# A fused attention and SwiGLU kernel whose whole instruction order is one list: another list of the same steps

## The chip, the cores and the metric

One core of one Trainium2 chip. The metric is the device time of one execution in microseconds (us). A core has five engines with an instruction stream each: TensorE (PE), VectorE (DVE), ScalarE (ACT), GpSimd (POOL) and SyncE (SP). Each runs its own stream in order and waits on semaphores for what it needs from the others; SP issues transfers, POOL does some elementwise work and issues others.

## The reference

Attention over selected blocks of keys, with a SwiGLU feed-forward network behind it. Batch 4, 8 heads, 768 positions, head size 64; then 3,072 tokens of width 512 and an inner width of 1,536.

```python
k_chunks = k.reshape(B, H, nc, chunk, D)                # chunk = 32, nc = 24
k_min, k_max = np.min(k_chunks, axis=3), np.max(k_chunks, axis=3)
ub = np.sum(np.maximum(q * k_min, q * k_max), axis=-1)  # per query and chunk
ub = np.where(causal, ub, -1000000000.0)
top_chunks = np.argsort(ub, axis=-1)[..., -6:]
scores = scale * np.matmul(q, k.transpose(0, 1, 3, 2))
mask = sel & (pos[:, None] >= pos[None, :])
attn = softmax(np.where(mask, scores, -1000000000.0))
x = np.matmul(attn, v)                                  # to (3072, 512)
xn = x / np.sqrt(np.mean(x * x, axis=-1, keepdims=True) + 1e-06) * rms_g
g = xn @ w_gate
out = (g * (1.0 / (1.0 + np.exp(-g))) * (xn @ w_val)) @ w_out
```

## The kernel before

The unit of the attention part is a pair: two heads of one batch element, 16 pairs in all, four to a batch element. The unit of the feed-forward part is half a batch element, 384 tokens, 8 halves in all. For a pair, k and q are loaded (`kload`, `qload`, L500, issued by SP into one of seven buffers `nat`), transposed on PE (`kT`, `qT`, L520, three tiles a step) and evicted by ACT or DVE (`kE`, `qE`, L290 and L294). DVE takes the minimum and maximum of each chunk of 32 keys (`kmn`, `kmx`, L551 and L549), a small step subtracts them (`dif`, L602), `relu` (L638, or L636 on ACT) makes the positive part of q, and PE forms the bounds (`ub`, L737 for the first six pairs, L795 for two pairs at once afterwards) and transposes them (`up`). DVE adds the causal mask (`ubm`), finds the largest values (`max`, L653) and writes the selection (`sel`, `grd`), which is appended to q as further rows: by a transposition on PE (`selT`, `selC`) for the first three pairs, by transposing DMAs of SP (`qX`, L560) for the others. Casts on POOL or ACT (`kC`, `qC`, `qN`, L294) put k and q in bf16 into one of three buffer sets. Then a pair has twelve score steps (`sc`, L882), an exponential for each on ACT (`exp`, L899), a causal mask on POOL where it is needed (`mask`, L905), the product with v (`av`, L918; v is loaded by POOL, L476) and the division (`xb`, L939).

When the four pairs of a batch element are done, its tokens are normalized (`sq`, `eps`, `root`, `xs`) and transposed: on PE for batch element 0 (`tp`, L1017), by DMAs of SP for the others (`xT`, L1006). Each half then has twelve `gate` steps (L1051) and twelve `val` steps (L1072) of four 128x384 matmuls each, with `tanh` (L1058), `tg` (L1064) and `hh` (L1080) behind them, and nine `po` steps (L1092) of four matmuls of 512 columns, evicted (`poE`) and stored (`out`, L1107). The weights come in six transfers that POOL issues: the first and the second half of the inner width of w_gate (`wg` 76 and 78) and of w_val (`wv` 77 and 79), and w_out (`wo` 80 and 81, L445). Gate and val steps of the first six of the twelve parts read the first half, those of the last six the second. Filler matmuls on zeros (`busy`, L339) may stand anywhere on PE; a list may leave them out.

What sets the order is neither the code's order nor a planner at build time. `add` only records a step, with the engines that it may take, what it depends on and which buffers it opens and uses; its number is the count of the steps recorded before it. Then `Order.run` goes through the string `PROGRAM`, and the steps are emitted as it says. A word is an engine's letter (P, A, D, G for POOL, S for SP), the step's number and, behind a colon, the buffer slots of what it opens: `P347:5,1` is step 347 on PE with PSUM banks 5 and 1. An engine's stream is the words with its letter, in the order of the list. A wait comes of dependencies and of buffers used again, so an instruction that has to wait holds up all that stands behind it on its engine.

Names with the step numbers that are spoken of below: `kload` 559 and 1105, `qload` 227 and 828; `qT` 228 and 230 (pair 2), `ub` 347 and `qX` 356 and 357 (pair 3); `kmn` 410, `kmx` 409, `dif` 411, `kC` 412 (pair 4); `kC` 554 and 555, `dif` 553 (pair 6); `qC` 237 (pair 2), `kC` 343 (pair 3); `gate` 1305 and 1315, `val` 1283, `tp` 1344 (batch element 0); `xT` 1520 (batch element 1); `busy` 28 and 29.

Of the kernel before, what the change touches and what calls it, by code (L numbers as in the profile page):

```python
# [28 lines left out]
    "S83:0 S88:1 S89 S82 D3 G0 D56 D55 D53 D54 D60 G63 A2 G65 P4:0 D59 P5:1 G66 P6:2 D58 P7:3 D57 G67 P8:4 S154:2 "  # L29
    "P9:5 G68 P86:6 S159:3 P10:7 G72 A87:0 P11:0 A69 D97:0 P92:1 D96:0 P12:2 G64 S335:4 G73 P84:3 D93:1 P90:4 A85 "  # L30
    "P13:5 P14:7 A91 P15:6 D95 P16:0 A99:0 P17:2 G101 D94 S222:5 P157:1 P155:5 D98 G62 A158:2 D103:3 P18:3 G61 "
    "P19:7 P20:4 S71 D156 P104:6,0 G102 D1 D52 D165:1 G168:1 P160:2 S330:6 A106:0 P162:3 D164:1 G74 A105 P21:1 "
    "A161:4 P107:7 A163 G167 P336:4 S70 D108:0 P338:5 A171:5 P22:0 G166 D109:2 P23:6 P24:1 A100 D110 S541:0 "
    "P172:2,3 A337:6 D112:0 A339 D111 P225:7 A173:0 D174 P113:0 G346:3 A226:1 S227:1 P175:6 A114 P223:1 D176:1 "
    "P25:4 P26:5 D177:3 P331:2 P333:3 D178 A224 G115:0 S404:2 P119:7 D332:2 A334 P147:6 A179:1 P135:4 D340:4 "
    "A148:0 G170 P128:5 P116:0 A136:1 D180 S399:3 P544:1 A117:2 D341:2 P150:3 P125:2 A545:0 P181:6 P141:4 A151:3 "
    "D232:5 A126:4 P138:0 G342 G236:2 P347:1,3 A120:5 D182 A129:6 G169 P228:2 A139:7 P230:7 S546:5 G183:1 D348:0 "
    "A349 P542:5 D229:5 A231 P350:6 D233:3 A142:8 P190:0 G345:0 P118:1 P121 A239:6 P144:3 P149:2 D351:2 P152 "
    "P184:7 G234 G235 A191:9 D352:6 P240:4,6 D543 A145:2 G238 D353 A185:5 P215:0 P122:5 G251:2 A241:0 D242 P143 "
    "A216:0 P146 P131:3 P243:7 A354 P405:4 A123:3 G237 D244:0 P209:6 P140 P137 A132:8 P218:0 D245:7 P193:7 A210:2 "  # L40
    "G358:3 P407:5 D406:3 A219:7 P203:3 A194:1 D246 P133 P124 P187:6 A408 D248:0 G247 P127 A204:8 P196:0 D153:0 "
    "P402:4 A188:3 P199:7 P217:5 P249:3 D355 A197:4 P130 P212:2 D250 S356:0 P211 A403:4 P195:6 G556:1 P206:0 "
    "A200:0 A213:6 P186 P400:4 G555:1 D134 A207:2 P264:7 P201 S357 P286:3 P214 P277:2 A265:1 G554 D401 P189 "
    "P258:0 P252:1 A278:5 D409:0 G343 P274:7 A259:0 S475:6 P261:4 A253:6 P205 D552:0 P192 G344 P198 P255:2 A275:3 "
    "P271:0 G415:1 D202 A256:8 S470:1 P267:1 P279:7 P220 P208 A287:9 A268:4 P266:2 D551:1 P283:6 A272:5 P288 "
    "P362:3 P257 P276 A262:7 P280:1 S75 D221 P269 P254 P369:0 P260 A281:2 P359:4 G412:2 D410:1 A370:1 P263 P282 "
    "A284:9 P273 P366:5 G76 D270 A363:8 P285 A360:3 P389:1 G77 P371:0 P364:6 P386:3 D329 A367:4 P361 P373:2 "
    "A390:6 G411 D365 G553 P368 P395:4 G78 A387:0 P471:5 D372 P416:7,1 D472:6 A1248:2,0 D1246:1 A1247:2 P379:6 "
    "P478:3 D418:0 A396:7 P547:0 D1249:3 D417 P27:5 A374:2 G1250:4 P397:1 D548:5 P392:4 P476:7 A380:5 P382:5 "
    "P473:2 D1251:0 A383:9 P391 P388 P376:0 A393:1 D1254:1 P375:6 P384 P1252:5 A479:2 P394 D1257:2 P381 A477 "  # L50
    "P1255:4 P419:3 A377:8 D398 G486:0 P1258:7 A1253:0 P378 D1259 P549:0 A1256 D385 P28:1 P29:5 A474 D420:1 "
    "P1260:7 A1336:5,0 D421:7 G413 P1280:1 A1335:1 D480:6 P1268:4 A1337:2 G414:0 D422 A1261:0 P1285:6 D1338:0 "
    "D423 A1281:1 D424 G1339:1 P1270:5 D1262:2 A1286:3 S426 D1282:4 P1275:2 A1271:5 D1346:3 P1263:3 A1276:6 S425 "
    "D1272:7 P1265:7 D1277:0 P1305:1 D1343:0 A1266:1 S559:0 P1288:5 D550 D1264:0 P1344:2 G557:3 P1315:0 D1287:5 "
    "A1345 S564:4 D1267:6 P439:3 A1316:2 P449:6 D1289:1 P445:2 P1300:7 A450:3 D1269:2 P1295:5 G427:0 A440:4 "
    "D481:2 A1301:3 P1283:6 A446:7 D1317:1 G79 A1296:5 P457:4 D1302:6 P560:3 A458:6 P436:2 G482 D1297:2 P1347:0 "
    "G81 A561:1 P562:7 D1348 P565:4 A563 D1284:3 P428:5 P463:3 A437:0 D1340:1 P432:0 G572:0 P487:7,6 A429:2 "
    "D570:3 A464:9 P1273:2 G451 A489:0 D488 A566:4 P1341:5 G485:0 P567:3 A1306:3 D1342 P459:6 A433:1 P490:7 "
    "D1274:4 G430 P1364:4 D569:2 G80 P466:5 P1349:0 A467:5 D491:0 P465 P442:2 D571 D568 P1399:5 A443:8 D1307:5 "
    "P460:7 P452 D575:2 A1400:4 P1278:3 A461:6 D1401:7 P577:2,1 A1350:3 D492:3 A1365:4 D493 G494 P453:7 P1308:5 "  # L60
    "A582:0 D578 A454:9 P1298:1 D1309:5 G455 P583:2 G484:2 D1299:6 P579:7 P462 D1366:5 P456 P1389:5 G434 D581:2 "
    "G483 D580:1 P468 P1392:1 D585 A1390:2 D584 D469:1 G573 P1310:4 D586:4 P1318:7 D592:5 D495 P1402:2 D1351:4 "
    "S496 P1374:6 D1279:7 D1391:3 P438:0 P1354:3 S497 D1393:8 P1303:5 D1403:9 A1355:0 P1367:1 A1375:2 D587 "
    "A1311:3 S700:3 D1319:10 P1290:2 G588 D1356:7 G498:1 P1379:7 D1312:1 A1291:0 P1293:3 D1368:11 A1380:3 G576:2 "
    "D1304:12 P524:4 P1325:1 D1292:5 A525:3 G574:0 D1294:13 P503:5 P444 D1381:6 P510:2 G526 P431 P447 P528:4 D593 "
    "A511:6 P1313:3 D589 A529:9 G594 P435 D1376:0 P703:7 S591 A504:5 P701:2 D1314:14 P1394:4 D595 D702:0 P537:6 "
    "P507:5 S590 P520:3 A538:0 D704 A1395:5 P1326 A521:8 D1396:3 P513:2 G522 S597 P1359:6 A514:2 P539:7 P441 "
    "P499:3 P1327 D448 A500:7 S596 A1360:2 P534:4 G501 P598:2 D1328:0 P1352:0 A535:1 G505 S682:1 A508:0 P516:3 "
    "P523 P506:1 D1353:15 P1384:4 A599:4 D1361:1 A517:8 P530 P536 P531:5 S705:5 D710:7 A1385:5 P512 P509 P665:0 "
    "A532:5 G714:2 P515 P678:2 P527 D1386:4 P672:3 A666:9 P518 P675:6 G558:3 D711:1 S841:2 P533 A673:1 P606:5 "  # L70
    "P502 P669:4 A679:6 P644:0 A676:0 D540 P661:3 G667 P1320:2 A607:2 G713 S823:0 D519 A662:3 P685:6 A670:8 "
    "P674:7 G663 P680 P623:5 D686:5 P657:3 P668 P683:1 G715:1 S687:6 A658:5 A645:7 P671 P1321 D684 A624:1 G646 "
    "D693:2 P648:4 G625 P651:6 S1329 P640:3 A649:6 P654:0 D692:0 P612:1 A641:9 P1322 A613:8 G642 P677 P706:5 "
    "D1323:1 G696:0 A655:0 P650:4 P842:3 S828:4 D707:3 A652:6 P647 P614:1 G712 P609:2 G600 P656 A843:4 P664 "
    "P626:0 P643 A610:7 P653 D681 G694 P633:5 S1324 P708:6 A634:8 P659 P615:3 P601 P826:2 A709 P611 P824:7 S846:3 "
# [1088 lines left out]
```

## Time and profile before

| | us |
|---|---|
| median of 3 runs | 312.94 |
| lowest and highest of them | 311.38, 313.39 |
| the profiled execution: its own time | 312.63 |
| the profiled execution: span from its first to its last instruction | 310.9 |

The granted TensorE clock was 0.999 in the profiled execution. The profile's groups give an instruction's line, engine, operation, what it writes and reads, shapes and count, then busy time and mean duration, then the idle time before it and what ended it. PE's matmuls are pipelined and their ends modelled, so their busy times overlap; the distance from one start to the next says what a step costs.

### The profile page before, as it was taken

Reading aid. Unit: us, or ns where it says so; the run is one execution under the profiler, and the core shown is the slowest. Engines: PE = TensorE matmul, PEld = TensorE weight load, DVE = VectorE, ACT = ScalarE, POOL = GpSimd, SP = SyncE. Lnnn points to the kernel's source line nnn. Section 1 sums busy time; section 2 is a strip of 40 time slices with the busy share of each in tenths; the row PEclk is TensorE's granted clock in tenths of the full one; section 3 lists DMA queues with packets and bytes.
Section 4 is the critical chain, followed back from the end, with each engine's and each line's share of the span. In section 5 each row is a group of like instructions: output and inputs, shape, how many; then the busy total and the mean of one; then the engine's idle time right before and its main releaser. Section 6 shows DMA issues by size and latency. Waiting matters only on the chain.

```text
span 310.9 us, 7415 instructions
## 1 busy us (share of the span) xinstructions
PE 300.8 (97%) x2764; PEld 190.4 (61%) x2782; DVE 232.2 (75%) x651; ACT 182.2 (59%) x405; POOL 119.5 (38%) x176
## 2 busy tenths in 40 slices
PE   7989998999999999999999999999999999999995
PEld 3657875666667764667776456666665455565542
DVE  5888988998977887789987897875743764477621
ACT  5789987672588763866997336667872303433110
POOL 8588856654547840632775104514030110000000
PEclk9999999999999999999999999999999999999999
DMA  9999999999999997996237136533000055200013
GB/s 172 221 170 175 121 209 209 158 168 150 154 176 206 201 163 145 231 163 165 55 26 50 33 74 178 53 74 29 3 0 2 34 86 186 102 2 0 0 70 136
DMA packets 113300, 35.35 MB, mean 114 GB/s; under 512 B 106224, under 2 KB 110064, under 8 KB 113264
## 3 DMA queue, kind: packets, MB, share of 16 engines
q1 hardware_dynamic: 83152, 26.62, 43.0%
q0 software_dynamic: 28512, 7.87, 25.4%
q10 hardware_dynamic: 1600, 0.39, 0.6%
q8 instruction: 22, 0.36, 0.5%
q14 instruction: 14, 0.11, 0.1%
HBM read 28.57 MB, written 6.29 MB: 112 GB/s over the span
## 4 chain that ended last, share of the span: by engine, by line
PE 87%; DMA 8%; POOL 2%; ACT 1%; issue 1%; ACTq 0%; SPq 0%; POOLq 0%
PE vp L1072 20%; PE po L1092 20%; PE gp L1051 19%; PE sc L882 10%; PE av L918 6%; DMA wg<-in_moe_w_gate_dram 5%; PE pq L520 3%; PE pk L520 3%; PE ub L795 2%; DMA knat<-in_k_dram 2%; PE ub L737 1%; DMA qnat<-in_q_dram 1%; POOL ke L294 1%; PE up L817 1%; PE busy L339 1%; POOL rt L638 1%
## 5 line engine op out<-in xcount | busy, mean ns | idle before, releaser
L899 ACT ACTIVATE pt<-sc 128x512 bf16<-128x512 f32 (+1 forms) x192 | 94.0, 556 | 21.2 <-PE sc L882 18.4
L1058 ACT ACTIVATE sg<-gp 128x384 bf16<-128x384 f32 x96 | 45.7, 495 | 72.2 <-PE gp L1051 62.6
L1072 PE MATMUL vp<-xT,wv 128*128 128x384 bf16 x384 | 74.4, 326 | 1.6 <-DMA wv<-in_moe_w_val_dram 1.5
L1051 PE MATMUL gp<-xT,wg 128*128 128x384 bf16 x384 | 74.2, 326 | 0.1
L1092 PE MATMUL po<-wo,hh 128*128 128x512 bf16 x271 | 66.8, 379 | 0.7
L1064 DVE SCALAR_TENSOR_TENSOR tg<-sg,gp 128x384 bf16<-128x384 bf16 x96 | 51.9, 549 | 20.6 <-ACT sg L1058 19.2
L1080 DVE TENSOR_TENSOR hh<-vp,tg 128x384 bf16<-128x384 f32 x96 | 51.5, 552 | 18.5 <-PE vp L1072 17.7
L882 PE MATMUL sc<-qs,ke 128*128 128x128 bf16 (+4 forms) x420 | 59.3, 251 | 0.0
L1072 PEld LDWEIGHTS <-wv 128*128 128x128 bf16 x384 | 35.8, 98 | 26.4 <-DMA wv<-in_moe_w_val_dram 1.8
L1051 PEld LDWEIGHTS <-wg 128*128 128x128 bf16 x384 | 35.7, 98 | 22.5 <-DMA wg<-in_moe_w_gate_dram 0.5
L1092 PEld LDWEIGHTS <-hh 128*128 128x128 bf16 x288 | 27.5, 98 | 27.5
L918 PEld LDWEIGHTS <-pt 128*128 128x128 bf16 x672 | 34.8, 98 | 11.1 <-POOL pt L905 0.3
L918 PE MATMUL av<-vx,pt 128*128 128x65 bf16 x672 | 41.2, 193 | 0.1
L905 POOL TENSOR_SCALAR_AFFINE_SELECT pt<-pt 128x512 bf16<-128x512 bf16 (+1 forms) x48 | 24.5, 522 | 38.5 <-ACT pt L899 38.1
L882 PEld LDWEIGHTS <-ke 89*128 89x128 bf16 (+1 forms) x420 | 31.0, 97 | 10.0 <-issue 1.4
L294 POOL CAST ke<-kt 64x768 bf16<-64x768 f32 x30 | 25.3, 846 | 7.3 <-PE sc L882 2.8
L987 POOL TENSOR_TENSOR ri<-ms,mhalf 128x3 f32<-128x3 f32 x8 | 7.2, 904 | 33.6 <-DVE ms L979 33.5
L995 DVE SCALAR_TENSOR_TENSOR xs<-xb,ri,gains 128x512 bf16<-128x512 bf16 x24 | 17.2, 751 | 3.1 <-POOL ri L987 2.9
L939 DVE TENSOR_TENSOR xb<-av,rden 128x384 bf16<-128x384 f32 (+1 forms) x34 | 18.2, 534 | 1.2
L520 PE MATMUL pk<-ident_f,knat 128*128 128x128 f32 x96 | 16.0, 282 | 1.7 <-DMA knat<-in_k_dram 1.7
L476 POOL DMA_DIRECT2D vx<-in_v_dram x16 | 17.3, 1079 | 0.1
L653 DVE MAX8 m<-ubm 128x8 f32<-128x8 f32 (+4 forms) x192 | 16.8, 160 | 0.2
(91 smaller groups left out, 300.6 us busy)
## 6 DMA issues: line engine op xcount, KB each, us to landing
out_dram<-osb SPq DMA_DIRECT2D x24, 256.0 KB, 2.3
knat<-in_k_dram SPq DMA_DIRECT2D x30, 192.0 KB, 4.4
qnat<-in_q_dram SPq DMA_DIRECT2D x30, 192.0 KB, 5.1
vx<-in_v_dram POOLq DMA_DIRECT2D x16, 192.0 KB, 5.9
wg<-in_moe_w_gate_dram POOLq DMA_DIRECT2D x2, 768.0 KB, 11.7
wv<-in_moe_w_val_dram POOLq DMA_DIRECT2D x2, 768.0 KB, 10.6
wo<-in_moe_w_out_dram POOLq DMA_DIRECT2D x2, 768.0 KB, 11.8
qs<-qn SPq DMA_TRANSPOSE x26, 2.8
```

What stands on the lines that cost most here:

```text
L294: engine[e].tensor_copy(out_, in_)
L520: nc.tensor.transpose(t[:, j * P:(j + 1) * P], nat[w].tile[:, j0 + j].rearrange("p h d -> p (h d)"), ident_f[:])
L882: nc.tensor.matmul(t[:, x:x + m, :].rearrange("p a b -> p (a b)"), ke[kk, kb * P:(kb + 1) * P], qs[kk, q0 * P:(q0 + m) * P], start=not tri ...
L899: nc.scalar.activation(out=t[:, 0:nn, :], in_=sc.tile[:, 0:nn, :], func=ACT.Exp, scale=SCALE)
L905: nc.gpsimd.affine_select(out=pt.tile[:, 0:nd, :], in_=pt.tile[:, 0:nd, :], compare_op=ALU.is_ge, fill=0.0, base=0, pattern=[[0, nd], [1, ...
L918: nc.tensor.matmul(av.tile[:, qi - i0, :], pt.tile[:, x, :], VX[c.v.slot][:, hl * NT + kb, :], start=(begin and m == 0), stop=(left[0] == ...
L1051: nc.tensor.matmul(t[:], wg[:, g, hs], XT[b].tile[:, g, cols], start=(g == 0), stop=(g == NP - 1))
L1058: nc.scalar.activation(out=t[:], in_=gp.tile[:], func=ACT.Tanh, scale=0.5)
L1064: nc.vector.scalar_tensor_tensor(out=t[:], in0=sg.tile[:], scalar=1.0, in1=gp.tile[:], op0=ALU.add, op1=ALU.mult)
L1072: nc.tensor.matmul(t[:], wv[:, g, hs], XT[b].tile[:, g, cols], start=(g == 0), stop=(g == NP - 1))
L1080: nc.vector.tensor_tensor(out=t[:], in0=vp.tile[:], in1=tg.tile[:], op=ALU.mult)
L1092: nc.tensor.matmul(po.tile[:], hhs[ht].tile[:, th * P:(th + 1) * P], wo[:, ht, :], start=(ht == 0), stop=(ht == NHT - 1))
```

## The change

`PROGRAM` is replaced by another list over the same recorded steps; nothing else in the file differs. The new list has 1,876 words, the old one 1,878: `busy` 28 and 29 are not in the new one, which leaves 24 fillers of 26. All other steps are in both. Steps that two engines may take are shared out anew in part: of the evictions `kE` ACT has 16 of 32 (was 19) and `qE` 21 (was 20), of `poE` 9 of 24 (was 12), of `ubE` 17 of 22 (was 12), of `sq` 18 of 24 (was 17), of `relu` 7 (was 6), and `grd` has 6 on ACT, 2 on DVE and 8 on POOL (was 3, 4 and 9). The slots of buffers differ throughout, and almost every line of the list does. Some lines of the two lists:

```diff
 PROGRAM = (
-    "S83:0 S88:1 S89 S82 D3 G0 D56 D55 D53 D54 D60 G63 A2 G65 P4:0 D59 P5:1 G66 P6:2 D58 P7:3 D57 G67 P8:4 S154:2 "
...
-    "D232:5 A126:4 P138:0 G342 G236:2 P347:1,3 A120:5 D182 A129:6 G169 P228:2 A139:7 P230:7 S546:5 G183:1 D348:0 "
...
-    "P402:4 A188:3 P199:7 P217:5 P249:3 D355 A197:4 P130 P212:2 D250 S356:0 P211 A403:4 P195:6 G556:1 P206:0 "
-    "A200:0 A213:6 P186 P400:4 G555:1 D134 A207:2 P264:7 P201 S357 P286:3 P214 P277:2 A265:1 G554 D401 P189 "
-    "P258:0 P252:1 A278:5 D409:0 G343 P274:7 A259:0 S475:6 P261:4 A253:6 P205 D552:0 P192 G344 P198 P255:2 A275:3 "
...
-    "P362:3 P257 P276 A262:7 P280:1 S75 D221 P269 P254 P369:0 P260 A281:2 P359:4 G412:2 D410:1 A370:1 P263 P282 "
-    "A284:9 P273 P366:5 G76 D270 A363:8 P285 A360:3 P389:1 G77 P371:0 P364:6 P386:3 D329 A367:4 P361 P373:2 "
-    "A390:6 G411 D365 G553 P368 P395:4 G78 A387:0 P471:5 D372 P416:7,1 D472:6 A1248:2,0 D1246:1 A1247:2 P379:6 "
...
-    "D1272:7 P1265:7 D1277:0 P1305:1 D1343:0 A1266:1 S559:0 P1288:5 D550 D1264:0 P1344:2 G557:3 P1315:0 D1287:5 "
...
-    "D481:2 A1301:3 P1283:6 A446:7 D1317:1 G79 A1296:5 P457:4 D1302:6 P560:3 A458:6 P436:2 G482 D1297:2 P1347:0 "
...
-    "D1431:3 P1372:5 D1398:21 P1409:7 S1432 D1388:22 D1373:23 P1419:6 D726 S1105:0 D733:5 P1414:1 D734 D725 P1420 "
...
-    "D1109:4 A1451:1 D1437:2 A754:6 P1416 S1520 A744:9 P755:2 P1106:5 G745 D1417:2 P816:3 G741 P746 S1128:0 "
...
+    "S83:0 S82 S89:1 S88 G0 D3 D55 D53 P4:0 D56 D60 P5:1 A2 G65 P6:2 D59 G64 P7:3 G61 G66 P8:4 S154:2 D52 D54 D57 "
...
+    "P181:1 A120:5 D341:2 P135:4 G169 P116:3 A136:6 D182 G342 P230:6 A123:7 G167 P228:4 S399:4 A231:5 D233:3 "
+    "P347:5,1 G236 A545:4 A229 D543 P184:6 G238 D239:3 A349:0 P138:0 A348 P209:4 G234 A185:8 P350:7 A210:9 P124:1 "
...
+    "P407:5 G354 P152 P215:0 D248:0 A213:4 P199:6 P137 G247 P400:4 A204:3 D408 P402:2 A401:6 D355 G555:0 P214:3 "
...
+    "A188:1 D153:0 P264:4 A207:9 G343:1 S357 S356 P217 P220 P261:0 D134 P267:5 P201:2 A265:2 P258:7 P252:6 G344 "
+    "A268:6 S475:5 D410:0 A259:7 P198 P286:4 P192 P208 P274:1 A253:4 P255:5 D409:0 A287:3 P277:7 A262:0 P260:6 "
+    "S470:6 P186 P266 A256:9 P189 D221 P280:4 G411 G415:0 A278:7 P362:0 P195 P257 P263 A275:8 P269 P366:5 D202 "
+    "S75 P547:3 A363:2 P369:7 A367:1 D551:1 P359:1 A370:5 P283:2 P368:0 G76 A360:9 D548:3 P371 P271:5 A284:0 "
+    "P279:7 G77 P288 P254 P364:1 A281:6 P361 P386:3 D365 A272:1 P382:2 G78 P282 P276 D270 P389:4 A387:5 P376:1 "
+    "P395:5 G412:2 A383:7 P285 D372 P273 P379:3 P392:6 D329 G554 P473:2 A380:3 P471:0 P416:3,7 A1248:2,0 D1247:1 "
...
+    "A1286:3 D1338:0 P1263:0 D1267:4 S426 G1339:2 A1261:5 D1287:6 P1283:3 D1262:7 P1270:6 S425 D1343:3 P1275:4 "
+    "D1346:0 A1271:0 P1344:5 D550 P1315:1 S559:0 A1345 D1284:0 G557:0 P1300:2 A1276:2 D1264:1 A1316:3 P1288:5 "
+    "D1277:5 S564:1 A1301:1 D1317:7 P445:3 P439:0 P1295:4 D1269:2 A440:0 G427:0 D1302:2 P1347:1 A446:1 P1305:7 "
...
+    "S1520 D1442:7 P785:2 D1462:1 P795:1 P792:3 P1415 D1412:0 A796:4 S1105:0 A786:6 D1422:1 P781:0 A793:2 P789:6 "
```

On POOL, the words ahead of the second transfer of gate weights (`G78`) are, from the cast of pair 6 on: before `G555 G554 G343 G344 G415 G412 G76 G77 G411 G553 G78`, after `G555 G237 G343 G344 G411 G415 G76 G77 G78`, with `G412` and `G554` behind. On PE, the steps from the first gate on are, before: gate 1260, 1280, val 1268, gate 1285, 1270, 1275, val 1263, gate 1265, 1305; after: gate 1280, 1260, 1265, 1285, val 1268, 1263, 1283, gate 1270, 1275, tp 1344, gate 1315. On DVE, between the selection of pair 3 and `kmx` 409, before: `selC` 250, `xb` 134, `kE` 401; after: `kE` 403, `selC` 250, `xb` 153 and 134, `kmn` 410. On SP, the k load 1105 stood directly behind the transposes of batch element 1's first half, and now stands behind `xT` 1520 of its second half and four `qX`.

222 rows, old and new, of the table PROGRAM are left out of this document.

## Prediction

> **What bounds the kernel now.** I read the page first, then TensorE's (PE's) waits, the windows (start and end, length, PE's busy time first), the chain of waits back from the end, and GpSimd's (POOL's) timeline at the place to which the chain leads.
>
> ```profile
> span 310.9 us, 7415 instructions
> ```
> ```profile
> PE pk L520 <- DMA knat<-in_k_dram: 1.7, 2, 1.3
> PE vp L1072 <- DMA wv<-in_moe_w_val_dram: 1.5, 1, 1.5
> PE busy L339 <- DVE zeros L334: 1.2, 1, 1.2
> PE pq L520 <- DMA qnat<-in_q_dram: 0.5, 1, 0.5
> PE pq L520 <- ACT pt L899: 0.2, 1, 0.2
> ```
> ```profile
> 0.00:57.00 57.00, 51.65 (x609) 35.46 (x611) 47.24 (x154) 45.57 (x101) 38.98 (x59) 1.00 1.22 179
> 57.00:307.00 250.00, 249.10 (x2157) 154.91 (x2171) 184.94 (x498) 136.08 (x303) 80.53 (x117) 1.00 0.58 97
> ```
>
> The two windows say where PE's time is lost: 249.1 of the 250 us from 57 to 307 are busy, against 51.65 of the first 57. All its waits together are 5.1 us, and the rows below put the wait for wv at 51.90, inside the first 57 us; the others there are for k and q as they come in. So there are two stages: a start that waits for transfers, and 250 us in which PE runs without a pause. In the second stage no order of the same work can gain anything; it can only add waits. What an order can gain is work that PE does before the second stage begins. The chain shows what starts that stage:
>
> ```profile
> 41.31 14.69 DMA wg<-in_moe_w_gate_dram
> 56.04 0.82 PE gp L1051 x4
> ```
> ```profile
> 57.52 0.22 PE tp L1017 x4
> 57.74 0.65 PE gp L1051 x4
> ```
> ```profile
> 33.05 3.35 POOL L294 CAST ke<-kt 64x768 bf16<-64x768 f32 x4 [1.06 <-PE sc L888]
> 36.49 2.14 POOL L638 TENSOR_SCALAR rt<-qt 128x768 f32<-128x768 f32 x1
> 38.57 0.82 POOL L294 CAST ke<-kt 64x768 bf16<-64x768 f32 x1
> 39.34 0.82 POOL L440 DMA_DIRECT2D wg<-in_moe_w_gate_dram  x1
> 40.17 0.75 POOL L440 DMA_DIRECT2D wv<-in_moe_w_val_dram  x1
> 40.92 0.45 POOL L602 TENSOR_TENSOR ku<-kmx,ku 128x24 f32<-128x24 f32 x2
> 41.31 0.79 POOL L440 DMA_DIRECT2D wg<-in_moe_w_gate_dram  x1
> ```
>
> The first two fences are the chain (start, length, what), the third is POOL. POOL is released by a score at 33.05, does four casts of k (0.84 us each), a ReLU and another cast, and only then issues the gate weights, the value weights and the second half of the gate weights. That third transfer takes 14.69 us and lands at 56.0; the first gate step that reads it starts at 56.04, and from there the chain stays on PE. PE meets the weights like this:
>
> ```profile
> 48.51 0.59 PE L339 MATMUL busy<-zeros 128*128 128x512 bf16 x2
> 48.99 1.46 PE L1051 MATMUL gp<-xT,wg 128*128 128x384 bf16 x8
> 51.90 0.82 PE L1072 MATMUL vp<-xT,wv 128*128 128x384 bf16 x4 [1.45 <-DMA wv<-in_moe_w_val_dram]
> 52.56 2.11 PE L1051 MATMUL gp<-xT,wg 128*128 128x384 bf16 x12
> ```
>
> Two filler matmuls, two gate steps of four matmuls, a wait of 1.45 us for wv, then a value step, three gate steps and two more steps up to the one on the late half of wg.
>
> **The change, part by part.** No instruction of the computation goes or comes. The program has 1,876 words instead of 1,878: fillers 28 and 29 are gone. Some eviction-like steps change between ScalarE (ACT) and VectorE (DVE); as PE had no wait for either after 57 us, I cost that at nothing there, the cover being the distance in PE's order between an exponential and its product, which is as short in both programs (the two at their shortest, by PE's own work, stand directly behind one another in both). If that cover fails it costs about one exponential each time, 556 ns:
>
> ```profile
> L899 ACT ACTIVATE pt<-sc 128x512 bf16<-128x512 f32 (+1 forms) x192 | 94.0, 556 | 21.2 <-PE sc L882 18.4
> ```
>
> *Work ahead of the late half of wg.* I compared the lists of PE's steps ahead of the first gate step on that half (step 1305 before, 1315 after). They are the same 172 steps, except that the two fillers are only in the old list, and that the new one has val 1283 and the transposition tp 1344 besides. A step of four 128x384 matmuls takes 0.65 us and a transposition of four 0.22 us (the chain's rows at 57.74 and 57.52). So if that gate step starts at the same 56.04, PE has 0.65 + 0.22 = 0.87 us less left to do. The two fillers are worth 48.99 - 48.51 = 0.48 us, but ahead of a wait: they bring PE to the weights earlier, not to the end.
>
> *Does PE get there in time?* In the new order four gates come first, then three vals, two gates and the tp: 9 x 0.65 + 0.22 = 6.07 us from the first gate to step 1315. With the first gate at 48.99 as before and no wait, 1315 would be reached at 55.06, 0.98 us ahead of the weights. The first value step now stands four steps behind the first gate, not two, which takes 2 x 0.65 = 1.30 of the 1.45 us of wv's wait. So the first gate may slip by 0.98 us before PE, not the weights, sets the end. Two edits can make it slip:
>
> ```profile
> 22.35 0.65 PE L737 MATMUL ub<-qt,ku 64*32 64x256 f32 x12
> 22.81 0.63 PE L737 MATMUL ub<-rt,ku 64*32 64x256 f32 x12
> 23.61 0.85 PE L520 MATMUL pq<-ident_f,qnat 128*128 128x128 f32 x6 [0.18 <-ACT pt L899]
> ```
>
> The bound of pair 3 (ub 347, at 22.35) used to run while PE waited for pair 2's q; now both transpositions of that q (qT 230, 228) stand ahead of it. What is behind on PE is everything, and the selection of pair 3 and its two transposing loads qX 357 and 356 hang on it. The ub rows last 1.0 us together from the first start to 23.4, so at that point PE falls back by up to 1.0 us; at the low end nothing, if q lands sooner. Two fillers fewer give 0.48 us back. I take a slip of 0.5 us, inside the cover of 0.98.
>
> *When do the weights leave?* On POOL, ahead of the weights, the chain's casts kC 554 and kC 412 (0.8 us each by their rows) are put behind the third transfer, as is dif 553; qC 237, another cast of the same size, and dif 411 come in ahead. kC 555 goes to another set of buffers, freed earlier, and the wait for a score is now at kC 343. From 33.05, POOL alone would have two casts, the ReLU and two issues, 1.7 + 2.1 + 1.6 = 5.4 us, and issue the third transfer at 38.5, against 41.31. But dif 411 waits for the maximum kmx 409 on DVE, and DVE does there:
>
> ```profile
> 31.70 0.61 DVE L668 SCALAR_TENSOR_TENSOR qn<-m,ubm 128x288 bf16<-128x288 f32 x1
> 32.34 1.14 DVE L294 COPY qs<-st 64x768 bf16<-64x768 bf16 x2
> 33.40 0.18 DVE L938 RECIPROCAL rden<-av 128x6 f32<-128x6 f32 x1
> 33.61 0.56 DVE L939 TENSOR_TENSOR xb<-av,rden 128x384 bf16<-128x384 f32 x1
> 34.09 0.55 DVE L294 COPY kt<-pk 128x384 f32<-128x384 f32 x1
> 34.74 0.95 DVE L549 TENSOR_REDUCE kmx<-kt 128x24 f32<-128x768 f32 x1
> 35.61 0.94 DVE L551 TENSOR_REDUCE ku<-kt 128x24 f32<-128x768 f32 x1
> ```
>
> After the selection (end 32.31) the new order has a copy kE (0.55), the copies selC (1.1), two norms xb (33.40 to 34.09, 0.69 each), kmn 410 and kmx 409 (0.9 each): 32.31 + 0.55 + 1.1 + 1.4 + 1.8 = 37.1. Then dif 411 (half of 0.45, 0.2), the ReLU (2.1) and the first issue at 39.4, against 39.34; the third, without the two difs between, at 41.0, against 41.31. So the casts taken away are replaced by a wait on DVE. For the landing I take 56.0 again: the bounds are 0.3 us earlier by the issue of the third and 1.0 us later if DVE is as late as PE can make it (below).
>
> ```profile
> DMA packets 4240, 3.28 MB, mean 193 GB/s; under 512 B 2574, under 2 KB 4110, under 8 KB 4238
> ...
> q0 software_dynamic: 1584, 2.36, 79.7%
> ```
>
> These two rows (transfers from 39 to 56 us) say why an earlier issue need not be an earlier landing: the three transfers, 2.36 MB, share 193 GB/s with the last k load, the gains and pair 4's transposes, and 2.36 MB at that rate are 12.2 us. The Trainium skill, DMA: Bandwidth & Descriptors, section Anatomy of one DMA, gives about 2.0 us plus the bytes over 436 GB/s for a transfer issued by GpSimd; as an estimate by that page three transfers of 768 KB would need 2.0 + 5.4 = 7.4 us, no weight would hold PE up, and the sum would be that of the faster rival below. The trace does not agree: 14.69 us.
>
> *Sum.* Start of the late gate step unchanged at 56.0: 0. Work left behind it: -0.87. One new wait of small size in the 250 us: +0.3 (bounds 0 and 3, below). The end is built alike: the last PE step is the last third of an output tile, evicted on ACT and stored. That gives -0.6 on the profiled execution's 312.63 us (span 310.9 and 1.7 around it), 312.0. The runs of before have a median of 312.94, 0.3 above the profiled one; I stay with 312.0.
>
> **Rivals.** *Faster: DVE is done in time and the transfers keep up.* Then the third transfer leaves up to 2.8 us earlier and PE itself is the limit, at 55.06 less the fillers' 0.48, 54.6: 1.46 + 0.87 = 2.3 us, 310.3. For it: the casts are really gone from the chain. Against: DVE's sum above, and the 193 GB/s.
>
> *Slower: the weights leave later because dif 411 holds them.* POOL is in order, and behind dif 411 stand the ReLU and all three transfers. Every microsecond that kmx 409 is later than 37.1 is one at the end, since nothing in the 250 us can take it back; it decides the sign from 37.1 + 0.87 = 38.0 on. A slip of pair 3's chain through PE by the 1.0 us above and again as much on DVE gives 2.0: 312.63 - 0.87 + 2.0 = 313.8.
>
> *Slower: short leads in the 250 us.*
>
> ```profile
> knat<-in_k_dram SPq DMA_DIRECT2D x30, 192.0 KB, 4.4
> ...
> xT<-xs SPq DMA_TRANSPOSE x18, 2.5
> ```
>
> Counting PE's work between a load's place and its first reader, k load 559 has 3.1 us, 1.1 less than before, k load 1105 has 3.9 (was 12.7, and now stands on SP's queue behind xT 1520, which waits for DVE), and the last xT of two halves 2.6. Against 4.4 and 2.5 us to landing these are waits of up to 1.3, 0.5 and twice 0.1, and as much again for what SP holds up behind them: about 3, so 315. Against it: other loads got longer leads (q load 828 11.7 us, was 7.2).
>
> *Nothing: the late gate step comes 0.87 us later for one of these reasons, and all is as it was,* 312.6.
>
> **How the numbers follow.** Forecast 0.45; faster rival 0.15; weights later 0.17; short leads 0.13; nothing 0.10. The range 310.4 to 314.6 leaves out about half of the short leads, the edge of the faster rival, and the tails of the rest, some 2 in 10. A measurement of this kernel can tell about 1% from no change: 309.8 to 316.1. Faster than that needs more than the whole start can give: 0.05. Slower needs short leads with more than three microseconds or two cases together: 0.09. Within: 0.86.
>
> **What would show it.** Right: PE's waits for wv nearly gone, the third weights transfer issued near 41 and landing near 56, no PE wait after it, and the PE window from 57 to the end as full as before. The faster rival shows as an issue near 38 and a gate on the late half before 55.5; the slower one as POOL idle ahead of ku L602 with a releaser on DVE, and an issue after 42. Short leads show as PE waits for knat or xT after 57. The prediction is wrong if PE has waits of over 2 us in all after 57, or if the late gate step starts 2 us from 56.

## The result and the profile after

| | before | after |
|---|---|---|
| median of 22 runs each, us | 312.35 | 313.94 |
| lowest and highest, us | 311.37, 313.91 | 312.61, 319.36 |
| profiled execution: its own time, span, us | 312.63, 310.9 | 313.27, 311.6 |

The ratio of after to before is 1.0051, 95% interval 1.003 to 1.0071: about half a per cent slower, and not the 0.2% faster that was forecast. Ratios here and below leave out runs more than 1.5% above the fastest of the same list (3 of the 22 after), medians and ranges do not; as such long runs come only with the short leads described below, the ratios of those lists understate their loss.

The two windows that carried the prediction, in the profile of after (start and end, length, then PE's busy time first):

```profile
span 311.6 us, 7411 instructions
```
```profile
0.00:57.00 57.00, 50.48 (x603) 35.31 (x606) 46.55 (x150) 43.82 (x98) 40.52 (x63) 1.00 1.10 176
57.00:307.00 250.00, 249.10 (x2160) 155.17 (x2174) 186.07 (x499) 139.26 (x311) 78.36 (x112) 1.00 0.57 99
```

The long stage is as full as before to the second decimal; in the profiled execution PE has no wait in it. The first 57 us have 1.17 us less work in them. PE's waits (us in total, times, longest), of which none lies behind 57:

```profile
PE pk L520 <- DMA knat<-in_k_dram: 3.8, 3, 2.7
PE busy L339 <- DVE zeros L334: 1.2, 1, 1.2
PE sc L882 <- DMA qs<-qn: 1.1, 1, 1.1
PE pq L520 <- DMA qnat<-in_q_dram: 0.2, 1, 0.2
```

The wait for wv is gone, as forecast. In its place stands a wait of 2.7 us for k. The sum of all waits is 6.3 us against 5.1; that is 1.2 us more, and with 0.48 us less of fillers the span should be 0.7 us longer, which it is. PE's timeline shows where:

```profile
45.46 0.85 PE L520 MATMUL pk<-ident_f,knat 128*128 128x128 f32 x6 [2.66 <-DMA knat<-in_k_dram]
...
51.36 2.76 PE L1051 MATMUL gp<-xT,wg 128*128 128x384 bf16 x16
53.95 2.11 PE L1072 MATMUL vp<-xT,wv 128*128 128x384 bf16 x12
55.90 1.46 PE L1051 MATMUL gp<-xT,wg 128*128 128x384 bf16 x8
57.20 0.39 PE L1017 MATMUL tp<-ident_b,xs 128*128 128x128 bf16 x4
57.43 1.46 PE L1051 MATMUL gp<-xT,wg 128*128 128x384 bf16 x8
```

The first row is `kT` 473 of pair 5, which reads `kload` 470. From there PE runs through: first gate at 51.36 (48.99 before), gate 1315 on the late weights at 57.43 (step 1305 at 56.04 before). The weights no longer set that step:

```profile
36.02 0.24 POOL L602 TENSOR_TENSOR ku<-kmx,ku 128x24 f32<-128x24 f32 x1 [2.17 <-DVE rden L938]
36.23 2.13 POOL L638 TENSOR_SCALAR rt<-qt 128x768 f32<-128x768 f32 x1
38.32 0.85 POOL L440 DMA_DIRECT2D wg<-in_moe_w_gate_dram  x1
39.16 0.76 POOL L440 DMA_DIRECT2D wv<-in_moe_w_val_dram  x1
39.89 0.77 POOL L440 DMA_DIRECT2D wg<-in_moe_w_gate_dram  x1
```

They leave at 38.32, 39.16 and 39.89, each 1.0 to 1.4 us earlier than before, and by the trace land at 47.77, 51.64 and 55.37, the last 2.06 us before it is read. The chain of waits (start, length, what) shows what sets the end instead:

```profile
32.79 0.23 PE sc L882 x2
33.02 0.83 POOL ke L294
33.86 0.22 SPq L560
...
34.12 1.66 SPq L560
...
37.04 0.54 SPq L500
...
37.63 7.70 DMA knat<-in_k_dram
45.33 0.14 issue
45.46 0.85 PE pk L520 x6
```

It is read upwards: PE waits for k load 470; its second DMA took 7.70 us; it left at 37.63 because the q load 475 and the transposes `qX` stand ahead of it on SP; and those waited for a cast on POOL and a score on PE. SP's own waits between 25 and 40 us name both:

```profile
SPq L560 <- DVE qn L668: 6.2, 1, 6.2
SPq L560 <- PE sc L882: 1.5, 1, 1.5
SPq L560 <- POOL ke L294: 1.1, 1, 1.1
```

In the profile of before the same stretch has a row for DVE alone (6.9 us). So two things are new: SP waits for a score and for a cast with the loads queued behind, and a load that takes 8.3 us from its first DMA's issue to its landing, where the same load, issued at the same 37.04, took 4.91 before. As the load itself leaves no later than before, what has changed for it is that the weights now follow 1.02 us sooner.

### The profile page after: what moved, and what is told of

It reads as the page before. It is cut to its first block, busy times and chain, and to the rows that moved or that the text cites. A ratio compares the mean times of both kernels' runs of the same rounds, so it can differ in the third digit from the quotient of the medians.

```text
span 311.6 us, 7411 instructions
## 1 busy us (share of the span) xinstructions
PE 299.8 (96%) x2761; PEld 190.5 (61%) x2780; DVE 232.8 (75%) x648; ACT 183.7 (59%) x409; POOL 118.9 (38%) x175
## 3 DMA queue, kind: packets, MB, share of 16 engines
HBM read 28.57 MB, written 6.29 MB: 112 GB/s over the span
## 4 chain that ended last, share of the span: by engine, by line
PE 88%; DMA 6%; SPq 4%; issue 1%; POOL 0%; DVE 0%; ACT 0%; ACTq 0%; DVEq 0%
PE vp L1072 20%; PE gp L1051 20%; PE po L1092 19%; PE sc L882 10%; PE av L918 6%; DMA knat<-in_k_dram 5%; PE pk L520 3%; PE pq L520 3%; SPq L500 2%; PE ub L795 2%; PE ub L737 1%; PE up L817 1%; SPq L560 1%; DMA out_dram<-osb 1%; PE tp L1017 0%
## 5 line engine op out<-in xcount | busy, mean ns | idle before, releaser
L1058 ACT ACTIVATE sg<-gp 128x384 bf16<-128x384 f32 x96 | 45.5, 492 | 61.7 <-PE gp L1051 52.7
L882 PE MATMUL sc<-qs,ke 128*128 128x128 bf16 (+5 forms) x420 | 57.8, 251 | 1.3 <-DMA qs<-qn 1.1
L1092 PEld LDWEIGHTS <-hh 128*128 128x128 bf16 x288 | 27.7, 98 | 28.1
L918 PEld LDWEIGHTS <-pt 128*128 128x128 bf16 x672 | 32.1, 98 | 9.2 <-ACT pt L899 0.4
L882 PEld LDWEIGHTS <-ke 128*128 128x128 bf16 (+1 forms) x420 | 30.9, 97 | 10.5 <-issue 1.8
L918 PE MATMUL av<-vx,pt 128*128 128x65 bf16 x672 | 37.2, 193 | 0.0
L296 DVE TENSOR_SCALAR osb<-po 128x512 f32<-128x512 f32 x15 | 10.2, 688 | 15.7 <-PE po L1092 12.1
```

The source lines that it names most:

```text
L882: nc.tensor.matmul(t[:, x:x + m, :].rearrange("p a b -> p (a b)"), ke[kk, kb * P:(kb + 1) * P], qs[kk, q0 * P:(q0 + m) * P], start=not tri ...
L918: nc.tensor.matmul(av.tile[:, qi - i0, :], pt.tile[:, x, :], VX[c.v.slot][:, hl * NT + kb, :], start=(begin and m == 0), stop=(left[0] == ...
L1058: nc.scalar.activation(out=t[:], in_=gp.tile[:], func=ACT.Tanh, scale=0.5)
L1092: nc.tensor.matmul(po.tile[:], hhs[ht].tile[:, th * P:(th + 1) * P], wo[:, ht, :], start=(ht == 0), stop=(ht == NHT - 1))
```

## The experiments

All ratios are to the kernel before, run beside the list on the same chip; the runs are from four chips, so two edits are compared through their ratios. There are 12 runs of each list unless another number is given. "Lead" is the time from the first DMA of k load 470 to the first weights transfer. Diffs show the words of one engine's stream around the edit. The first run is the changed list once more.

> The changed list as it is, beside the kernel before on the same chip. Expected by every theory: ratio 1.003 to 1.007, PE's wait at the transposition kT 473 (reads k load 470) 2 to 3 us, first gate step near 51.4, late gate step 1315 near 57.4.

Ratio 1.005 (1.0011 to 1.009); median 318.28, from 313.27 to 321.76. By the medians the loss is 1.6%. The wait is there, but in the profiled execution, which is the longest of the 12, it is 7.5 us and not 2 to 3, and the first gate comes later than expected. The wide range is taken up again at the end.

**470 far ahead of the weights.**

```diff
-S399:4 S357 S356 S475:5 S470:6 S75
+S399:4 S475:5 S470:6 S357 S356 S75
```

> The changed list with the q load 475 and the k load 470 put ahead of the transposes qX 357 and 356 on SP, where SP idles from 25 to 32.7 us. Nothing else moves. Theory A (the loss is PE's wait for k load 470, which lands only at 45.3): the load lands before 32, the wait of 2.7 us at kT 473 goes, the first gate step comes near 48.7 and the late gate step 1315 near 55.4, where the third weights transfer becomes the limit; 2.0 us below the changed list, ratio to the kernel before 0.993 to 0.999. Rival B (470's wait only covers other late inputs, so that PE is held up elsewhere in the first 57 us by as much): first gate step within 0.5 us of 51.4, ratio near 1.005. Rival C (the earlier loads take bandwidth from the v loads and qX): new waits of 1 us and more ahead of 38 us, and less than half of the 2.0 us gained.

Ratio 1.0017 (0.9991 to 1.0043). The wait at 473 is gone, but the first gate comes at 51.40, where rival B puts it, and the late one at 57.47. PE's waits name rival C as the reason: `av L918 <- DMA vx` 0.9 us and `sc L882 <- DMA qs` 1.9 us. The loads left at 25.1 to 27.7, among the three v loads of POOL (25.5 to 27.6). v load 183 landed 1.4 us later, PE stood still for it, the scores that `qX` waits for came later, `qX` left at 34.12, and 473 was reached only at 44.63. An idle stretch of a queue is not an idle stretch of what it feeds.

**The weights 0.9 us later.**

```diff
-G411 G415:0 G76 G77 G78 G412:2 G554
+G411 G415:0 G554 G76 G77 G78 G412:2
```

> The changed list with the cast kC 554 put back ahead of the first weights transfer on POOL, as in the list before: the three weights transfers leave about 0.85 us later (39.2, 40.0, 40.7). Theory A1 (k load 470 is late because the weights' transfers now start 1 us earlier, within half a microsecond of its second DMA, and their traffic is served ahead of or beside it): 470 lands near 42.5 instead of 45.3, PE's wait at kT 473 shrinks from 2.7 to below 0.6 us, the late weights land near 56.2 and set the late gate step; 1.2 us below the changed list, ratio 0.998 to 1.002. Rival A2 (470 is late for another reason, such as its buffer, its place on SP's queue or qX beside it): it lands again at 45 to 45.5, and the time is that of the changed list, ratio 1.003 to 1.007.

Ratio 1.0022 (1.0 to 1.0045). A1's mechanism holds: with a lead of 1.72 instead of 1.28 us, 470 lands 4.92 us after its issue, and the first gate comes at 49.87. The size does not: the third weights transfer lands at 57.38 and not at 56.2, and now holds PE:

```profile
49.87 2.76 PE L1051 MATMUL gp<-xT,wg 128*128 128x384 bf16 x16
...
57.43 1.47 PE L1051 MATMUL gp<-xT,wg 128*128 128x384 bf16 x8 [1.30 <-DMA wg<-in_moe_w_gate_dram]
```

**470 ahead of 475, the gains out of the way, and both.**

```diff
-S399:4 S357 S356 S475:5 S470:6 S75
+S399:4 S357 S356 S470:6 S475:5 S75
```

> The changed list with the k load 470 put directly ahead of the q load 475 on SP (both still behind the transposes qX 357 and 356), so that its two DMAs leave at 35.8 and 36.5, more than 1.5 us ahead of the weights. Theory Z (from 39 to 56 us the DMA engines are full at about 210 GB/s, so that what k and q get the weights lose): PE's wait of 2.7 us for knat at kT 473 goes, the first gate step comes at 48.8 to 49.9, but the third weights transfer lands at 56.5 to 57.4 instead of 55.4 and sets the late gate step there; 0 to 0.9 us below the changed list, ratio 1.001 to 1.004. Rival P (the order of the loads alone matters, the weights keep their landing of 55.4): late gate step 55.4, ratio 0.997 to 1.000. Rival Q (the q load 475 takes 470's place as the late one): a wait of 0.5 us or more at its transposes.

```diff
-S399:4 S357 S356 S475:5 S470:6 S75
+S399:4 S75 S357 S356 S475:5 S470:6
```

> The changed list with the load of the gains (256 KB, step 75) put ahead of the transposes qX 357 and 356 on SP, where SP idles from 25 to 32.7 us; it leaves the stretch in which weights and k load 470 move. Theory Z: 256 KB are 1.2 us at 210 GB/s; 470 and the weights land 0.5 to 1.2 us earlier together, the first gate step comes near 50.4, the late gate step near 56.4; 1.0 us below the changed list, ratio 1.000 to 1.003. Rival R (470 is late by its place behind the weights' packets, not by the sum of the bytes): it lands at 45.0 to 45.6 again, and the time is that of the changed list, 1.004 to 1.006.

```diff
-S399:4 S357 S356 S475:5 S470:6 S75
+S399:4 S75 S357 S356 S470:6 S475:5
```

> Both of the two other edits: gains ahead of the transposes, k load 470 directly ahead of q load 475. Theory Z: the wait at kT 473 goes and 256 KB less are moved with the weights; first gate step near 48.8, late gate step near 55.4, so that the work of 0.87 us done ahead of it comes out as a gain: ratio 0.995 to 0.999, about 2 us below the changed list. Rival (sum not limited by DMA but by PE's slip ahead of 38 us, the wait of 1.1 us for qs at sc 362): late gate step at 56.4 or later, ratio 1.001 or more.

Ratios 1.0037 (1.0009 to 1.0065), 1.0035 (1.0006 to 1.0065) and 1.0018 (0.9991 to 1.0045). The first went as theory Z says, with the weights even later than its 56.5 to 57.4: 470 on time, first gate at 49.59, weights at 57.73. In the second 470 landed at 45.68, as rival R says, though the gains were no longer beside it, and PE stood 1.5 us at 473 until then; with the gains in the stretch of the v loads PE also waited for vx (0.6) and `qX` left at 34.14. In the third 475 took 470's place (8.14 us to landing with a lead of 0.63), and PE, not the weights, was late: 1.7 us for qs, 0.9 for vx, late gate 57.02. So in all five of these edits the late gate stayed between 57.0 and 57.8; behind each wait taken away stood another. (One of the 12 runs of the second took 633 us; nothing here explains it.)

**The order of the feed-forward steps alone, in the list before.**

```diff
-P1260:7 P1280:1 P1268:4 P1285:6 P1270:5 P1275:2 P1263:3 P1265:7 P1305:1 P1288:5 P1344:2 P1315:0
+P1260:7 P1280:1 P1285:6 P1270:5 P1268:4 P1275:2 P1263:3 P1265:7 P1288:5 P1344:2 P1305:1 P1315:0
```

> The list before with one part of the change alone, the order of PE's feed-forward steps: the value step 1268 is put behind the gate step 1270, so that four gates stand ahead of it, and the gate step 1305 on the late weights behind val 1288 and the transposition tp 1344. Theory (the step of the prediction: work of 0.87 us is done ahead of the late weights, in the time of wv's wait): wv's wait falls from 1.45 to some 0.3 us, 1305 starts near 56.0 with 0.87 us less left, ratio 0.996 to 0.999. Rival (PE was the limit there, and the moved work only delays 1305): 1305 near 56.8, ratio 0.999 to 1.002.

Ratio 0.9984 (0.9964 to 1.0005), median 0.83 us lower: consistent with a gain of 0.87 us, without excluding none. The trace shows the step: no wait for wv is left, and 1305 starts at 55.23, 0.14 us behind the landing of its weights, and not near 56.0 as expected. It also shows a part handed back, 1.9 us of waits behind 57 in an execution that was the slowest of its 12:

```profile
PE sc L882 <- ACT pt L899: 0.7, 1, 0.7
PE av L918 <- DMA vx<-in_v_dram: 0.5, 1, 0.5
PE pq L520 <- DMA qnat<-in_q_dram: 0.5, 1, 0.5
PE sc L882 <- DMA qs<-qn: 0.2, 1, 0.2
```

**The same order with the gains moved, and the gains alone, in the list before.** The first has the edit above besides this one:

```diff
-S356:0 S357 S475:6 S470:1 S75
+S75 S356:0 S357 S475:6 S470:1
```

> The list before with the order of PE's feed-forward steps changed as in the run of that part alone, and the load of the gains put ahead of the transposes qX 356 and 357. Theory Z: weights land 1 us earlier, no wait for wv or wg is left, PE sets the late gate step at 54.5 to 55.0; ratio 0.994 to 0.998. Rival G (what PE gains at the start is handed back to loads of 57 to 150 us whose landing does not move with it): waits of 1 us and more after 57, ratio 0.998 to 1.000 like the run without the gains moved.

> The list before with one edit: the load of the gains (256 KB) put ahead of the transposes qX 356 and 357 on SP. It separates the two parts of the run in which this edit and the order of the feed-forward steps stood together (0.9952). Theory Z (bytes that leave the stretch from 39 to 56 us bring the weights in earlier): wv's wait falls from 1.45 us to about 0.3 and the late weights land near 54.8; 0.6 to 1.2 us gained, ratio 0.996 to 0.998. Rival (the gains are no part of the weights' 14 us): no change, 0.999 to 1.001, weights at 55.5 to 56.5.

Ratios 0.9952 (0.9927 to 0.9977) and 0.9935 (0.9907 to 0.9964): both faster than the list before. In this list v load 183 leaves at 22.5, well ahead of the gains, so that nothing is held up. wv's wait is 0.2 us in the run of the gains alone, with the late weights at 55.50 rather than the 54.8 expected. The gain of the gains alone (9 runs) is larger than the 0.2 to 0.4% expected; its profiled span, 310.6 us against 310.9 before, shows only a part of it, so where the rest comes from stays open. That run against the one with both edits cannot be told apart by these intervals.

**The order undone, in the changed list.**

```diff
-P1263:0 P1283:3 P1270:6 P1275:4 P1344:5 P1315:1
+P1263:0 P1270:6 P1275:4 P1315:1 P1344:5 P1283:3
```

> The changed list with val 1283 and tp 1344 put behind the gate step 1315, that is without the work of 0.87 us that the prediction counted as a gain. Theory I (in the changed list PE, not the third weights transfer, sets the late step: no wait of PE stands behind kT 473 at 45.5, so the order of its steps behind that is worth nothing): 1315 starts 0.87 us earlier, near 56.6, with 0.87 us more left, ratio as the changed list's, 1.003 to 1.007. Rival (the step still gains its 0.87 us in the changed list): 0.9 us slower than the changed list, ratio 1.006 to 1.010.

Ratio 1.0076 (1.0035 to 1.0117), which doesn't tell the two apart. The trace agrees with theory I: from the first gate at 51.84 PE runs without a wait to 1315 at 57.03 (expected near 56.6), 5.19 us instead of 6.07, with 0.87 us more left behind it. The first gate was 0.5 us later than the changed list's for other reasons (waits for vx and q).

**The wait on SP: which buffer set pair 3 has.** Pair 3's `qX` writes into a set that its cast `kC` 343 or `qX` itself opens: set 0 in the list before, whose last readers are the scores of pair 0, and set 1 in the changed one, read by the scores of pair 1.

With the sets, the casts 343 and 555 trade places on POOL, and later openings of the two sets are exchanged too.

```diff
-G555:0 G237 G343:1 G344
+G343:0 G237 G555:1 G344
...
-G573:1
+G573:0
...
```

> The changed list with two buffer sets exchanged: pair 3 takes set 0 (last read by the scores of pair 0) and pair 6 set 1, instead of 1 and 0, with the casts kC 343 and kC 555 in each other's place on POOL; later openings of the two sets are exchanged too. In the changed list the transposes qX 357 and 356 have their input at 31.1 but wait 1.5 us more for the scores of pair 1 that read set 1, and hold SP's queue with k load 470 in it. Theory S (that wait is the root: SP is late by it, and 470 so runs into the weights): qX leaves near 31.3, the wait of 1.1 us for qs at sc 362 goes, k load 470 leaves near 35.6 and lands by 41, PE's wait at kT 473 goes or is below 0.5 us; first gate step 48.5 to 49.5, late gate step 55.4 to 56.4; ratio 0.996 to 1.001, 1 to 2 us below the changed list. Rival (the loads and the weights still share the DMA engines, and the weights then land late): 470 on time, but the third weights transfer lands at 57 or later, ratio 1.002 or more.

Ratio 0.9933 (0.9905 to 0.996); median 311.43, and 1.2% below the changed list by the two ratios. SP's queue and PE in its profile:

```profile
31.70 2.64 SPq L560 DMA_TRANSPOSE qs<-qn  x2
34.38 2.00 SPq L500 DMA_DIRECT2D qnat<-in_q_dram  x2
36.43 1.22 SPq L500 DMA_DIRECT2D knat<-in_k_dram  x2
```
```profile
42.33 0.82 PE L520 MATMUL pk<-ident_f,knat 128*128 128x128 f32 x6
...
49.09 2.76 PE L1051 MATMUL gp<-xT,wg 128*128 128x384 bf16 x16
51.69 2.11 PE L1072 MATMUL vp<-xT,wv 128*128 128x384 bf16 x12
53.64 1.46 PE L1051 MATMUL gp<-xT,wg 128*128 128x384 bf16 x8
55.33 1.48 PE L1051 MATMUL gp<-xT,wg 128*128 128x384 bf16 x8
```

`qX` leaves 1.05 us earlier (not the 1.4 expected), 470 with a lead of 2.30 us, and it lands in 4.54 us. Of the 1.02 us by which this lead is longer than the changed list's, 0.61 come from 470 (36.43 instead of 37.04) and 0.41 from the weights, which leave later (38.73 instead of 38.32). SP's waits between 25 and 40 us still name a score and a cast, for less time:

```profile
SPq L560 <- PE sc L882: 1.2, 1, 1.2
SPq L560 <- POOL qs L294: 0.6, 1, 0.6
```

So the run shows what a longer lead is worth; it does not tell the set from the place of the two casts. There is no wait at 473, the first gate is at 49.09, and the late one starts with the landing of its weights at 55.33, with the 0.87 us done ahead of it. That is the forecast's mechanism: 0.87 us less left, and the late gate, which the forecast left where it was, 0.7 us earlier than the 56.04 before, 1.6 us together; its profiled span is 1.3 us shorter, 309.6 against 310.9.

**All of it together.** The run before, with `S75` ahead of `S357`, `S470` ahead of `S475`, and on POOL:

```diff
-G167 G236 G238 G234 G183:1
+G167 G183:1 G236 G238 G234
```

> The run with the two sets exchanged, and three edits more: gains ahead of the transposes, k load 470 ahead of q load 475, and the v load 183 two casts earlier on POOL (near 22.7 instead of 25.1), so that the gains don't hold it up. Theory S with Z: no wait over 0.5 us for qs, vx, knat or weights from 22 us on, first gate step 48 to 48.8, late gate step 54.0 to 55.0; ratio 0.990 to 0.996. Rival (the next limit is close behind, PE's and DVE's chain to the first gate): late gate step 55.4 or later, ratio 0.997 or more.

Ratio 0.9945 (0.9921 to 0.997): no better than the exchange of sets alone. The ratio lies in the theory's range, but the late gate is where the rival puts it: the weights land at 54.81, and PE reaches it only at 55.62.

**The lead alone, in the list before.** The two lists differ almost everywhere, so one edit shortens the lead alone, by putting two casts behind the weights:

```diff
-G555:1 G554 G343 G344 G415:1 G412:2 G76 G77 G411 G553 G78
+G555:1 G343 G344 G415:1 G76 G77 G411 G553 G78 G412:2 G554
```

> The list before, with the casts kC 412 and kC 554 put behind the third weights transfer on POOL as in the changed list, and nothing else: the first weights transfer leaves near 37.7 instead of 39.3, 0.7 us behind the first DMA of k load 470 (2.3 us in the list before). Theory C (a k or q load that leaves less than about 1.3 us ahead of the weights lands 7 us and more after its issue instead of 4 to 5): 470 lands at 44 to 46, PE's wait at kT 471 grows from 0.4 us to 2 to 4 us, the first gate step comes near 51 and the late gate step at 56 to 57 although the weights left earlier; ratio 1.000 to 1.006, slower runs among them. Rival D (it is the changed list's other order on SP and PE that makes 470 late): 470 lands near 42, the weights land 1.5 us earlier, wv's wait of 1.45 us goes; ratio 0.994 to 0.997.

Ratio 1.0217 (1.0167 to 1.0268; 6 runs, 11 of the list before): theory C, and far above its size. No wait of PE names the two casts. The weights left at 36.69, a lead of 0.29 us, and 470 landed 12.85 us after its issue:

```profile
49.38 0.87 PE L520 MATMUL pk<-ident_f,knat 128*128 128x128 f32 x3 [8.66 <-DMA knat<-in_k_dram]
```

So letting the weights go 2.65 us earlier cost the list before 2.2%. The leads and landings in these traces, in us:

| run | lead of 470 | 470, issue to landing | third weights transfer, issue to landing |
|---|---|---|---|
| lead shortened in the list before | 0.29 | 12.85 | 15.89 |
| order undone | 0.76 | 7.77 | 15.87 |
| changed list again | 0.85 | 13.11 | 16.31 |
| gains moved in the changed list | 0.97 | 7.07 | 16.16 |
| changed list | 1.28 | 8.29 | 15.47 |
| weights later | 1.72 | 4.92 | 16.54 |
| gains alone, list before | 1.77 | 4.89 | 14.55 |
| both edits, list before | 2.00 | 4.76 | 13.69 |
| 470 ahead of 475 | 2.28 | 4.01 | 17.84 |
| list before | 2.30 | 4.91 | 14.69 |
| sets exchanged | 2.30 | 4.54 | 14.97 |

With a lead of up to 1.28 us the load takes 7 to 13 us, from 1.72 us on 4 to 5; no run lies between. It is the second of the load's two DMAs that is late: in the changed list the first took 4.1 us and the second 7.7. Not in the table are three runs with leads of 1.85, 2.45 and 4.35 us (3.98, 4.97 and 5.07 us to landing) and the first edit, where 470 took 10.99 us among the v loads, far from the weights.

## Why the prediction was wrong

In the prediction's sum, the term "start of the late gate step unchanged" stood at 0 and came to +1.39 (57.43 against 56.04); the 0.87 us came as counted; the new wait in the 250 us, put at +0.3, came to 0. That makes +0.5, and the two profiled executions are 0.64 us apart. Of the signs that the prediction named for being right, four came: wv's wait gone, a landing near 56, no PE wait after 57, a window as full as before. None of the four is on PE's way to the first gate, and there it failed.

**The bound: right.** 249.1 of 250 us are busy after 57 in both lists, with no wait in the profiled execution of after. The short leads in that stage, the slower rival at 315, did not show there.

**The work ahead of the late gate: right as work, not a gain by itself.** The 0.87 us are real where the weights set the late step (sets exchanged: 55.33 with the weights' landing). In the changed list PE sets it, 2.06 us behind the weights, and then the order of PE's steps from 45.5 on is worth nothing. The prediction stated that condition and believed it met.

**"The first gate may slip by 0.98 us ... I take a slip of 0.5 us, inside the cover": this is the step that failed.** The slip was 51.36 - 48.99 = 2.37 us. It did not come from the two edits that the prediction named (the bound behind two transpositions, two fillers): with the wait for 470 gone the first gate came at 49.09, 49.55, 49.59 and 49.87 in four runs, slips of 0.1 to 0.9, within the cover (in two others, the first edit and the one with both moves on SP, waits for v and `qX` took its place). It came from k load 470, which the prediction did not cost at all. Its row of 193 GB/s named "the last k load" among those that share with the weights, and was read in one direction only: what the load does to the weights, not what the weights do to the load. In the profile of before that load is read 0.13 us after it lands.

**When the weights leave: wrong by 1.1 us, the other way.** 39.4 and 41.0 were forecast for the first and the third, 38.32 and 39.89 came (39.29 and 40.87 in the changed list run again, but there 470 too left 1.40 us later, at 38.44). The sum on DVE began at the selection's end of before, 32.31; after had the selection done at 31.1, and `kmx` 409 ended at 35.86 instead of 37.1. So the faster rival's condition that DVE is done in time was met in part (the third transfer left 1.42 us earlier, not 2.8), and the outcome was the opposite: the earlier weights shortened the lead from 2.30 to 1.28 us. Of the rival "`dif` 411 holds the weights" the first sign is there, POOL idle for 2.17 us ahead of `ku` L602 with a releaser on DVE; its second, an issue after 42, did not come, so it did not make the weights late.

**The landing at 56.0 with bounds of 0.3 and 1.0: about right for the changed list (55.37), wrong as bounds.** 55.37 is itself just outside them (55.7 to 57.0), and in two runs in which 470 came through beside the weights the third transfer landed at 57.38 and 57.73. The estimate of 7.4 us for the three transfers counted 768 KB each, which is what they write, in bf16. They read f32: the profile's page gives 28.57 MB read from HBM, and q, k and v (18.87), the gains (0.26) and all weights make this up only with four bytes a weight (9.44). With the 4.72 MB that the three read, the estimate's two terms give 2.0 + 10.8 = 12.8 us, an estimate again, not far from the 14.69.

**Not on the list of steps: the buffer slot.** The prediction saw that the wait for a score is now at `kC` 343 and followed it on POOL alone. The same set has `qX` as a writer, so the same wait stands on SP, with three loads behind it. It held SP for 1.5 us, but 470 still left at the same 37.04 as before; only with the weights 1.02 us earlier did that become a loss. Exchanging the two sets (`G343:1` and `G555:0`), and with them the places of the two casts, takes the loss away: that list is 0.7% faster than the one before. How much of this is the set and how much the place, no run separates.

## What to carry to other kernels

When a load is issued in the last microseconds ahead of a large transfer on another queue, its lead over that transfer is a quantity of its own: write it down for before and after, and treat "this transfer now leaves earlier" as a risk for every small load beside it. For a step that is moved or given another buffer, list every engine that writes into that buffer, queues included; a wait shows up on each of them, and what stands behind it on an in-order queue is late as well. And sum PE's idle time, not one chain's end: a gain behind the place where PE waits last is worth nothing until that wait is gone.

## What the runs showed of the hardware

**Two queues are served packet by packet.** From 40 to 46 us of the run with the shortened lead, the rows of the two queues (packets, MB, share of 16 engines) are:

```profile
q0 software_dynamic: 655, 0.98, 92.9%
q1 hardware_dynamic: 622, 0.16, 20.0%
```

and from 37 to 40 us of the run with the sets exchanged, where SP's queue is alone:

```profile
q1 hardware_dynamic: 2727, 0.70, 107.8%
```

Beside the weights the small packets of k (0.16 MB in 622, some 257 bytes each) come at the rate of the weights' packets (0.98 MB in 655, 1.5 KB each): about one for one, and one seventh of the bytes. That is 104 packets a microsecond against 909 alone. In these 6 us, what of the load had not moved when the weights began thus crawled at the pace of the weights' packets. The Trainium skill, DMA: Bandwidth & Descriptors, section Queues, rings and completion order, says that a DMA engine goes round the queues that have work, a packet at a time; the trace agrees, by the two counts, if the profile's packets are what the page calls one. In the changed list's first profile much less was left: from 42 to 45.4 us no more than 26 packets under 512 B moved, beside 283 of the weights' queue, and yet the load landed only at 45.33. One of 16 engines would move about 22 in that time at 104 a microsecond for all, so a single engine that was behind would do; this is an estimate, as the rows don't tell the engines apart. Why the weights themselves take 1 to 3 us longer in most of these runs, also in two where 470 came through, no run settles; in those two the gains left at the same time as the first weights transfer or 0.1 us behind it.

**A long wait also costs clock.** The windows of 38 to 57 us in the run with the shortened lead (PE idle for 8.66 us), and in the changed list run again (7.51 us), with the granted clock behind the five busy times:

```profile
38.00:57.00 19.00, 10.34 (x131) 7.41 (x129) 7.78 (x21) 7.49 (x20) 3.92 (x7) 0.73 0.91 162
```
```profile
38.00:57.00 19.00, 10.64 (x134) 7.87 (x134) 8.73 (x22) 8.98 (x21) 6.34 (x8) 0.73 1.00 181
```

The granted clock is 0.73 there and 1.00 in the changed list's first profile, where the wait was 2.66 us. It is a stretch of some 10.2 us at 0.50: from 44.2 to 54.4 us in the first of the two and from 46.5 to 56.8 in the second. It begins 3.5 and 2.4 us after PE's wait began and ends 5.1 us after PE started again, so that on top of the wait PE lost some 2.5 us of work (an estimate: half of 5.1).

The longest runs fit this. The changed list run again has six runs above 318 us, with a granted clock of 0.983 to 0.989, and six below, with 0.995 to 1.000; the one with the trace, 321.76 us, has 0.983. Runs above 316.1 us occur in the lists of the table with a lead of up to 1.28 us, and once where 475 had taken 470's place; none of the other lists, the one before among them, has one. But a run without a trace has only its time and its clock, so that 470 came late in each of them is argued and not shown.
